# Narrow scores for the second half of the keys in a retention and MoE kernel, and the turns of two units moved

## The chip, the cores and the metric

The kernel runs on one core of a Trainium2 chip. The core has five engines with a queue each: TensorE (PE, matmuls, whose weight loads are listed apart as PEld), VectorE (DVE), ScalarE (ACT), GpSimd (POOL) and SyncE (SP, which here only issues DMAs). DMA transfers are carried out by 16 DMA engines, whichever queue issued them. The metric is the device time of one execution in microseconds (us), as the median of several; lower is better.

## The reference

The reference computes a retention layer and, on its result, a two-layer network with the ELU function between the layers.

```python
scores = scale * np.matmul(q, k.transpose(0, 1, 3, 2))       # q, k, v: 8 batches, 8 heads, 576 tokens, 64 wide
rel = pos[:, None] - pos[None, :]
Dmat = np.where(rel >= 0, gamma[:, None, None] ** rel[None, :, :], 0.0)
ret = np.matmul(scores * Dmat[None], v)                      # each query sees only keys at or before it
...
h = x @ w_in                                                 # x: ret as 4608 tokens x 512; w_in 512 x 2048
g = np.where(h > 0.0, h, np.exp(np.minimum(h, 0.0)) - 1.0)
out = g @ w_out                                              # w_out 2048 x 512
```

What matters for the change is the mask: a key that lies after a query contributes nothing to it.

## The kernel before

**Units.** The 4608 tokens are cut into 36 units of 128 tokens. Nine units cover two batches, so that the unit with `u % 9 == 4` holds the last 64 tokens of one batch and the first 64 of the next. The decay factors are split in two, one multiplied onto v (`scale_v`, on GpSimd, line 183) and one multiplied onto the result (`put_x`, on VectorE, line 316). What is left of the decay matrix inside a unit is a triangle of ones, and what earlier units contribute goes through a running state of 64 x 64 per head.

**Steps of a unit.** `load_v` and `load_qk` fetch the inputs. `turn(u)` transposes queries and keys so that the head width lies on the partitions. For units below `PE_TURNED` (8 of them) it does so with eight TensorE transposes into the buffer of the pool `ps_s`, from which VectorE copies one half (line 205) and ScalarE the other (line 206); for later units it is one DMA transpose on the SP queue (line 208). `scores(u)` (line 220) multiplies keys with queries, 16 matmuls in four groups, one for each pair of heads `hp`. The four matmuls of a group belong to the two heads `i` (rows 0 to 63 or 64 to 127 of the array) and the two halves `j` of the keys (columns 0 to 63 or 64 to 127). `masks(u)` (line 232) multiplies the scores with the triangle on VectorE. `inter(u)` (line 254) adds what the state contributes, `intra(u)` (line 303) what the unit's own keys contribute, `state(u)` (line 270) forms the unit's own addition to the state, and `state_out` (lines 285 to 295) adds it to the running sum on VectorE and casts it on ScalarE. These products share one buffer `o` of the pool `ps_o`, which there is once; the scores of a unit share the one buffer of `ps_s` with the transposes. `put_x` writes the unit's input of the network.

**The network.** Units are put together to groups: [0, 1, 2], [3], [4], [5], [6, 7], [8, 9], [10, 11, 12], [13, 14, 15] and fours after that. `ffn1` (called `f1`) computes one or more tiles of the first layer (line 382) into one of three buffers of `ps_h`. ELU is made by three engines in turn: the exponential e on ScalarE (line 387), m on GpSimd (line 389), and g on VectorE (line 347), which also frees the `ps_h` buffer. `ffn2` computes a quarter of an output tile (line 407).

**Order.** The order on each engine is that of the program text (`manual_schedule`), and only data and buffers make an engine wait. Up to unit 5 the order is written out by hand. After that a list of slots (tiles of `f1` and quarters of `ffn2`) is walked, and events are put between them by due times: `stretch(u)` (scores of the next unit, then `inter`, `intra`, `state` of the next unit, `put_x`), the turn of unit u + 3, and the loads of unit u + 5. A slot counter goes on with each slot (`tick`); things in `todo` are run when the counter has reached their number, and the g operations are run up to three slots late (`finish`). `dummy(n)` is n matmuls of 512 columns on a constant tile whose result is not used.

Of the kernel before, what the change touches and what calls it, by code (L numbers as in the profile page):

```python
# [9 lines left out]
FP32 = mybir.dt.float32  # L10
# [7 lines left out]
def kernel(  # L18
# [9 lines left out]
    nc = tc.nc  # L28
# [4 lines left out]
    P = 128  # L33
    HP = H // 2
# [8 lines left out]
    GROUPS += [list(range(u, u + 4)) for u in range(16, NU, 4)]  # L43
    NG = len(GROUPS)
    group_of = {u: (g, i) for g, us in enumerate(GROUPS) for i, u in enumerate(us)}
    PE_TURNED = 8

    def place(u):

# [22 lines left out]
    ps_s = ctx.enter_context(tc.tile_pool(name="ps_s", bufs=1, space=PSUM))  # L72
# [53 lines left out]
    for h in range(H):  # L126
        b, j = divmod(h, KJ)
# [40 lines left out]
    def dummy(n):  # L168

        if n:  # L170
            dum = ps_m.tile([P, 512], FP32, name="dum", tag="pm")
        for _ in range(n):
            nc.tensor.matmul(dum, warm[:, :P], warm, start=True, stop=True)  # L173


    qkTs, vns, scs, pts, os_, sbs, sts, sums = {}, {}, {}, {}, {}, {}, {}, {}

    def scale_v(u, half=None):

        if u not in vns:  # L180
            vns[u] = nat.tile([P, H, D], BF16, name="vn", tag="vn")
        h0, h1 = (0, H) if half is None else (half * HP, half * HP + HP)
        nc.gpsimd.tensor_tensor(  # L183
            vns[u][:, h0:h1], raws[u][:, h0:h1],
            gk[:, u % R, h0:h1].unsqueeze(2).to_broadcast([P, h1 - h0, D]), ALU.mult,
        )

    def turn(u, bank=None, keys_on_v=False, between=0):

        t = tpool.tile([P, 2, HP, P], BF16, name="qkT", tag="qkT")  # L190
        n = kns[u]
        c_v = 1 if keys_on_v else 0
        if u < PE_TURNED:
            if bank:
                pool, tag = bank
                ps = [pool.tile([P, HP, P], BF16, name="tr", tag=tag) for c in range(2)]
            else:
                both = ps_s.tile([P, 2, 2, HP, P], BF16, name="tr", tag="sc")
                ps = [both[:, c, 0] for c in range(2)]
            for c in range(2):  # L200
                if c:
                    dummy(between)
                for hp in range(HP):
                    nc.tensor.transpose(ps[c][:, hp], n[:, c, 2 * hp : 2 * hp + 2].rearrange("p h d -> p (h d)"), ident)  # L204
            nc.vector.tensor_copy(t[:, c_v], ps[c_v])
            nc.scalar.copy(t[:, 1 - c_v], ps[1 - c_v])  # L206
        else:
            nc.sync.dma_start_transpose(
                t.rearrange("p c h t -> p (c h) t"), n.rearrange("p c h d -> p (c h d)")
            )  # L210
        qkTs[u] = t

    def scores(u):
        t = qkTs[u]
        sc = ps_s.tile([P, 2, HP, P], FP32, name="sc", tag="sc")
        for hp in range(HP):
            for j in range(2):
                for i in range(2):
                    r = slice(i * D, (i + 1) * D)
                    nc.tensor.matmul(  # L220
                        sc[j * 64 : (j + 1) * 64, i, hp], t[r, 1, hp, j * 64 : (j + 1) * 64], t[r, 0, hp],
                        start=(hp == 0), stop=(hp == HP - 1), skip_group_check=True,
                    )
        scs[u] = sc

    def masks(u, i=None):

        if u not in pts:
            pts[u] = ppool.tile([P, 2, HP, P], BF16, name="pt", tag="pt")
        m = mask[:, 1 if u % R == 4 else 0]  # L230
        s = slice(0, 2) if i is None else slice(i, i + 1)
        nc.vector.tensor_tensor(  # L232
            pts[u][:, s].rearrange("p i h t -> p (i h) t"), scs[u][:, s].rearrange("p i h t -> p (i h) t"),
            m.unsqueeze(1).to_broadcast([P, (s.stop - s.start) * HP, P]), ALU.mult,
        )
# [5 lines left out]
    def inter(u):  # L241

        if u not in os_:
            os_[u] = ps_o.tile([P, 2, 512], FP32, name="o", tag="o")
        o = os_[u]
        r = u % R
        if r == 0:
            return
        n = 64 if r == 4 else P
        for a in range(2):  # L250
            for b in range(2):
                for i in range(2):
                    rows = slice(i * D, (i + 1) * D)
                    nc.tensor.matmul(  # L254
                        o[b * D : (b + 1) * D, i, a * P : a * P + n], sbs[u][rows, 2 * b + a],
                        qkTs[u][rows, 0, 2 * b + a, :n],
                        start=(a == 0), stop=False, skip_group_check=True,
                    )

    def state(u, beside):  # L260

        r = u % R
        if r == 8:
            return
        sts[u] = os_[beside][:, 1 if r == 4 else 0, 256:512].rearrange("p (c d) -> p c d", c=HP)
        rows = slice(64, P) if r == 4 else slice(0, P)
        for hp in range(HP):
            for i in range(2):
                h = 2 * hp + i
                nc.tensor.matmul(  # L270
                    sts[u][i * D : (i + 1) * D, hp], kns[u][rows, 1, h], vns[u][rows, h],
                    start=(hp == 0), stop=(hp == HP - 1), skip_group_check=True,
                )

    slot = [0]
    todo = []

    def state_out(u, cast_later=False):
        r = u % R
        if r == 8:  # L280
            return
        s = ppool.tile([P, HP, D], BF16, name="sb", tag="sb")
        sbs[u + 1] = s
        if r in (3, 7):
            nc.vector.tensor_tensor(s, sts[u], sums[u - 1], ALU.add)
            return
        sums[u] = ppool.tile([P, HP, D], FP32, name="sum", tag="sum")
        if r in (0, 4):
            nc.vector.tensor_copy(sums[u], sts[u])
        else:  # L290
            nc.vector.tensor_tensor(sums[u], sts[u], sums[u - 1], ALU.add)
        if cast_later:
            todo.append((slot[0] + 1, lambda: nc.scalar.copy(s, sums[u])))
        else:
            nc.scalar.copy(s, sums[u])

    def intra(u):
        o = os_[u]
        for a in range(2):
            for i in range(2):  # L300
                for b in range(2):
                    h = 4 * b + 2 * a + i
                    nc.tensor.matmul(  # L303
                        o[b * D : (b + 1) * D, i, a * P : (a + 1) * P], vns[u][:, h], pts[u][:, i, 2 * b + a],
                        start=(u % R == 0 and a == 0), stop=(a == 1), skip_group_check=True,
                    )
# [3 lines left out]
    def put_x(u):  # L310
        g, i = group_of[u]
        if i == 0:
            xts[g] = xpool.tile([P, KJ, 512], BF16, name="xt", tag="xt")
        r = u % R
        s0 = P * r if r < 5 else 64 + P * (r - 5)
        nc.vector.tensor_tensor(  # L316
            xts[g][:, :, i * P : (i + 1) * P].rearrange("p (a i) t -> p a i t", a=2), outputs(os_[u]),
            gx[:, :, s0 : s0 + P].rearrange("p (a i) t -> p a i t", a=2), ALU.mult,
        )

    def stretch(u, ahead=True):

        ahead = ahead and u + 1 < NU
        if ahead:
            scores(u + 1)
        inter(u)
        intra(u)
        if ahead:
            state(u + 1, u)
        put_x(u)  # L330
        if u + 2 < PE_TURNED:
            masks(u + 1)
        elif ahead:
            todo.append((slot[0] + 1, lambda: masks(u + 1)))
        if ahead:
            todo.append((slot[0] + 3, lambda: state_out(u + 1, True)))

# [5 lines left out]
    def finish(n=0):  # L343

        while late and late[0][0] <= slot[0] - n:
            _, gt_, ph, m, _ = late.pop(0)
            nc.vector.scalar_tensor_tensor(gt_, ph, 0.0, m, ALU.max, ALU.min)  # L347
# [129 lines left out]
    for u in range(2):  # L477
# [7 lines left out]
        state_out(u)  # L485
        dummy(2)
    scores(2)
    masks(2)
    dummy(4)


    def f1(g, n, bank=None):
        k = 512 // (P * len(GROUPS[g]))
        ffn1(g, k * n, bank)
# [61 lines left out]
    scores(5)  # L556
    state(5, 4)
    masks(5)
    f1(2, 0)
    f1(2, 1)  # L560
    finish(1)
    turn(6)
    scale_v(7)
    f1(2, 2)
    state_out(5)
# [32 lines left out]
    for u in range(5, NU):  # L598
        def at(share):
            return due[u] + share * (due[u + 1] - due[u])  # L600
        events.append((due[u], 0, u))
        if u + 2 < PE_TURNED:
            events.append((at(0.5), 1, u + 2))
# [7 lines left out]
    for f, g, s, d in slots:  # L611
        while events and events[0][0] <= now + d / 2:
            _, kind, u = events.pop(0)
# [13 lines left out]
    u = NU - 1  # L627
# [31 lines left out]
```

## Time and profile before

| | |
|---|---|
| time, median of 6 runs | 311.94 us (311.4 to 312.97) |
| the profiled execution | 312.79 us, of which the span of the profile is 311.0 us |
| busy in the span | PE 302.3, POOL 202.2, DVE 179.7, ACT 124.6, PEld 164.9 us |
| scores, L220 PE | 576 matmuls of 64 x 128, 15.0 us busy |
| transposes, L204 PE | 64 matmuls, 5.2 us busy |
| dummies, L173 PE | 34 matmuls, 11.0 us busy |
| DMA transposes, L208 SP | 28, median 4.7 us from issue to landing |

In the profile L220 is line 220 of the kernel. "pt<-sc,mask" reads: the operation writes `pt` and reads `sc` and `mask`. A timeline row has its start, the time that the row takes, the engine, the line, the operation, and in brackets how long the engine was idle before and what ended the idle time. A row of waits has the total, the number of times and the longest. A row of windows has the stretch, its length, the busy time and number of instructions of each engine named, the granted clock of TensorE as a share, the DMA busy time in the stretch and the rate in GB/s. Busy times of single matmuls overlap, since matmuls are pipelined.

### The profile page before, as it was taken

The numbers are of one execution on the slowest core, as the hardware profiler recorded it, in microseconds if no ns is written. First come the engines' busy times: TensorE is split into PE (matmuls) and PEld (weight loads), VectorE is DVE, ScalarE is ACT, GpSimd is POOL, SyncE is SP. The second block draws the span as 40 slices with busy tenths as digits, with TensorE's granted clock in tenths as the row PEclk, the third lists the DMA queues.
The fourth block names the chain that finished last, engine by engine and source line by source line (L and its number), as shares of the span: only waits on it lengthen the run. The fifth ranks groups of instructions, "written<-read, shape, count | busy, mean of one in ns | idle before, by whom it ended". The sixth has DMA issues, their size and how long they took to land.

```text
span 311.0 us, 7378 instructions
## 1 busy us (share of the span) xinstructions
PE 302.3 (97%) x2938; PEld 164.9 (53%) x2938; DVE 179.7 (58%) x305; ACT 124.6 (40%) x229; POOL 202.2 (65%) x292
## 2 busy tenths in 40 slices
PE   8897999899999999999999999999999999999995
PEld 3474746677666555555454444444444444444444
DVE  4657615776776666666666565666666665434300
ACT  5344413434434452344444433444334433444311
POOL 8886794899977778787777666766664433333300
PEclk9999999999999999999999999999999999999999
DMA  9999999799999999999999999999995200001111
GB/s 157 190 203 205 153 168 233 99 168 179 205 173 190 134 119 169 155 146 138 142 169 116 135 134 134 138 130 136 135 137 84 70 36 35 34 36 40 63 70 67
DMA packets 150882, 40.59 MB, mean 131 GB/s; under 512 B 141824, under 2 KB 146304, under 8 KB 150848
## 3 DMA queue, kind: packets, MB, share of 16 engines
q0 software_dynamic: 77264, 13.64, 56.0%
q1 hardware_dynamic: 72144, 24.19, 42.0%
q10 hardware_dynamic: 1440, 2.29, 2.2%
q8 instruction: 23, 0.38, 0.5%
q14 instruction: 11, 0.09, 0.1%
HBM read 36.70 MB, written 9.44 MB: 148 GB/s over the span
## 4 chain that ended last, share of the span: by engine, by line
PE 87%; DMA 6%; POOL 3%; DVE 1%; issue 1%; ACT 1%; POOLq 0%; DVEq 0%; ACTq 0%
PE ph L382 37%; PE pm L407 34%; PE pm L438 4%; PE o L303 4%; PE sc L220 4%; DMA w_in_sb<-in_moe_w_in_dram 4%; DMA qkn<-in_k_dram 3%; PE o L270 1%; POOL qkn L93 1%; PE pmh L423 1%; PE o L254 1%; PE tr L204 1%; POOL m L389 0%; DVE g L347 0%; DVE pt L232 0%
## 5 line engine op out<-in xcount | busy, mean ns | idle before, releaser
L389 POOL TENSOR_SCALAR m<-e 128x512 bf16<-128x512 f32 (+1 forms) x156 | 91.1, 586 | 89.2 <-ACT e L387 81.9
L382 PE MATMUL ph<-xt,w_in_sb 128*128 128x512 bf16 (+3 forms) x808 | 141.5, 313 | 2.2 <-DMA w_in_sb<-in_moe_w_in_dram 1.8
L387 ACT ACTIVATE e<-ph 128x512 f32<-128x512 f32 (+1 forms) x156 | 87.5, 564 | 137.6 <-PE ph L382 132.3
L347 DVE SCALAR_TENSOR_TENSOR g<-ph,m 128x512 bf16<-128x512 f32 (+1 forms) x156 | 99.7, 647 | 62.1 <-POOL m L389 61.8
L407 PE MATMUL pm<-w_out_sb,g 128*128 128x512 bf16 x496 | 125.5, 379 | 0.2 <-ACT ot L414 0.2
L382 PEld LDWEIGHTS <-w_in_sb 128*128 128x128 bf16 x808 | 69.2, 98 | 54.2 <-issue 3.0
L407 PEld LDWEIGHTS <-g 128*128 128x128 bf16 x496 | 48.0, 98 | 53.1 <-issue 0.4
L316 DVE TENSOR_TENSOR xt<-o,gx 128x512 bf16<-128x512 f32 x36 | 24.9, 691 | 39.6 <-PE o L270 30.6
L232 DVE TENSOR_TENSOR pt<-sc,mask 128x1024 bf16<-128x1024 f32 (+1 forms) x37 | 43.9, 1187 | 3.9 <-PE sc L220 3.9
L183 POOL TENSOR_TENSOR vn<-rv,gk 128x512 bf16<-128x512 f32 (+1 forms) x37 | 37.8, 1021 | 0.0
L93 POOL DMA_DIRECT2D qkn<-in_q_dram x39 | 35.1, 901 | 0.7 <-DVE pt L232 0.4
L93 POOL DMA_DIRECT2D qkn<-in_k_dram x39 | 33.3, 855 | 1.2 <-DMA qkn<-in_k_dram 1.2
L414 ACT COPY ot<-pm 128x512 f32<-128x512 f32 x31 | 18.1, 585 | 14.1 <-PE pm L407 14.1
L220 PEld LDWEIGHTS <-qkT 64*64 64x64 bf16 x576 | 9.2, 106 | 14.1 <-issue 10.8
L220 PE MATMUL sc<-qkT 64*64 64x128 bf16 x576 | 15.0, 222 | 0.9 <-ACT qkT L206 0.8
L303 PE MATMUL o<-pt,vn 128*64 128x128 bf16 x288 | 14.9, 225 | 0.0
L438 PE MATMUL pm<-w_out_sb,g 128*128 128x512 bf16 x64 | 14.5, 379 | 0.0
L173 PE MATMUL dum<-warm 128*128 128x512 bf16 x34 | 11.0, 457 | 1.2 <-DVE warm L119 1.2
L206 ACT COPY qkT<-tr 128x512 bf16<-128x512 bf16 x8 | 4.7, 583 | 15.5 <-DVE rv L82 10.7
L303 PEld LDWEIGHTS <-vn 128*64 128x64 bf16 x288 | 9.1, 109 | 3.0
L438 PEld LDWEIGHTS <-g 128*128 128x128 bf16 x64 | 6.1, 98 | 6.6
L270 PE MATMUL o<-vn,qkn 128*64 128x64 bf16 (+1 forms) x256 | 9.5, 196 | 0.0
(49 smaller groups left out, 98.1 us busy)
## 6 DMA issues: line engine op xcount, KB each, us to landing
rv<-in_v_dram SPq DMA_DIRECT2D x31, 256.0 KB, 4.9
out_dram<-ot SPq DMA_DIRECT2D x27, 256.0 KB, 2.4
qkn<-in_q_dram POOLq DMA_DIRECT2D x31, 128.0 KB, 5.0
qkn<-in_k_dram POOLq DMA_DIRECT2D x31, 128.0 KB, 5.4
w_in_sb<-in_moe_w_in_dram POOLq DMA_DIRECT2D x8, 256.0 KB, 9.3
w_out_sb<-in_moe_w_out_dram POOLq DMA_DIRECT2D x2, 1024.0 KB, 16.8
out_dram<-ot ACTq DMA_DIRECT2D x8, 256.0 KB, 3.9
rv<-in_v_dram SPq DMA_DIRECT2D x8, 128.0 KB, 5.4
```

What stands on the lines that cost most here:

```text
L93: nc.gpsimd.dma_start(kns[u][p0 : p0 + n, c], (q, k)[c][b, :, s0 : s0 + n, :].rearrange("h p d -> p h d"))
L183: nc.gpsimd.tensor_tensor(vns[u][:, h0:h1], raws[u][:, h0:h1], gk[:, u % R, h0:h1].unsqueeze(2).to_broadcast([P, h1 - h0, D]), ALU.mult,)
L220: nc.tensor.matmul(sc[j * 64 : (j + 1) * 64, i, hp], t[r, 1, hp, j * 64 : (j + 1) * 64], t[r, 0, hp], start=(hp == 0), stop=(hp == HP - 1) ...
L232: nc.vector.tensor_tensor(pts[u][:, s].rearrange("p i h t -> p (i h) t"), scs[u][:, s].rearrange("p i h t -> p (i h) t"), m.unsqueeze(1).t ...
L303: nc.tensor.matmul(o[b * D : (b + 1) * D, i, a * P : (a + 1) * P], vns[u][:, h], pts[u][:, i, 2 * b + a], start=(u % R == 0 and a == 0), s ...
L316: nc.vector.tensor_tensor(xts[g][:, :, i * P : (i + 1) * P].rearrange("p (a i) t -> p a i t", a=2), outputs(os_[u]), gx[:, :, s0 : s0 + P] ...
L347: nc.vector.scalar_tensor_tensor(gt_, ph, 0.0, m, ALU.max, ALU.min)
L382: nc.tensor.matmul(ph[:, i * n : (i + 1) * n], w_in_sb[:, j, f : f + P], xts[g][:, j, :n], start=(j == 0), stop=(j == KJ - 1), skip_group_ ...
L387: nc.scalar.activation(e[:, w], ph[:, w], AF.Exp)
L389: nc.gpsimd.tensor_scalar(m[:, w], e[:, w], -1.0, 1.0, ALU.add, ALU.mult)
L407: nc.tensor.matmul(pm, gts[g, ft][:, it * P : (it + 1) * P], w_out_sb[:, ft], start=(ft == 0), stop=(ft == NFT - 1))
L438: nc.tensor.matmul(acc[u], gts[g, ft][:, it * P : (it + 1) * P], w_out_sb[:, ft], start=(ft == 0), stop=(ft == NFT - 1))
```

## The change

`PE_TURNED` goes from 8 to 7. From unit 7 on, the scores of all units use one buffer of `ps_s` that is kept; its corner for the second 64 keys and the first 64 queries is zeroed once by VectorE (`keep_scores`, two slots after the stretch of unit 5). The matmuls of the second 64 keys are given the last 64 queries alone, so that eight of the 16 matmuls of a unit have 64 columns instead of 128. The mask of unit 6 is put one slot later. In the part written by hand, the turn of unit 6 is placed one slot sooner, between the two first tiles of group 2, and the turn of unit 7, which was an event after the stretch of unit 5 with TensorE transposes, becomes a DMA transpose ahead of the first of these tiles. Of four dummies after the mask of unit 2, one stays.

```diff
-    PE_TURNED = 8
+    PE_TURNED = 7
...
     def scores(u):
         t = qkTs[u]
-        sc = ps_s.tile([P, 2, HP, P], FP32, name="sc", tag="sc")
+        narrow = u >= PE_TURNED
+        if narrow:
+            sc = scs[PE_TURNED]
+        else:
+            sc = ps_s.tile([P, 2, HP, P], FP32, name="sc", tag="sc")
         for hp in range(HP):
             for j in range(2):
                 for i in range(2):
                     r = slice(i * D, (i + 1) * D)
+                    c = slice(j * 64 if narrow else 0, P)
                     nc.tensor.matmul(
-                        sc[j * 64 : (j + 1) * 64, i, hp], t[r, 1, hp, j * 64 : (j + 1) * 64], t[r, 0, hp],
+                        sc[j * 64 : (j + 1) * 64, i, hp, c], t[r, 1, hp, j * 64 : (j + 1) * 64], t[r, 0, hp, c],
                         start=(hp == 0), stop=(hp == HP - 1), skip_group_check=True,
                     )
         scs[u] = sc
+
+    def keep_scores():
+
+        scs[PE_TURNED] = ps_s.tile([P, 2, HP, P], FP32, name="sc", tag="sc")
+        nc.vector.memset(scs[PE_TURNED][64:P, :, :, 0:64], 0.0)
...
         elif ahead:
             todo.append((slot[0] + 1, lambda: masks(u + 1)))
+        if u + 2 == PE_TURNED:
+            todo.append((slot[0] + 2, keep_scores))
         if ahead:
             todo.append((slot[0] + 3, lambda: state_out(u + 1, True)))
...
     scores(2)
     masks(2)
-    dummy(4)
+    dummy(1)
...
     masks(5)
+    turn(7)
     f1(2, 0)
+    turn(6)
     f1(2, 1)
     finish(1)
-    turn(6)
     scale_v(7)
```

## The prediction

> **What bounds the kernel now.** I read the chain that ended last first, then TensorE's waits.
>
> ```profile
> PE 87%; DMA 6%; POOL 3%; DVE 1%; issue 1%; ACT 1%; POOLq 0%; DVEq 0%; ACTq 0%
> ```
>
> ```profile
> PE ph L382 <- DMA w_in_sb<-in_moe_w_in_dram: 1.8, 1, 1.8
> ...
> PE sc L220 <- ACT qkT L206: 0.8, 1, 0.8
> PE tr L204 <- DMA qkn<-in_k_dram: 0.7, 1, 0.7
> PE ph L382 <- DVE g L347: 0.4, 1, 0.4
> ```
>
> After about 30 us the end is set by TensorE (PE) working without pause; its named waits come to some 5 us, most of them early. So an edit counts if it shortens TensorE's own sequence after 30 us or removes a wait there. Hence three places: the scores of each unit, the dummies near 16 us, the turns of units 6 and 7 near 55 us.
>
> The scores of unit 24, in stretches of 56 ns, line 220 alone (microseconds, TensorE's busy time and matmuls touched, then weight loads):
>
> ```profile
> 169.62:169.70 0.08, 0.07 (x4) 0.07 (x8) 1.00 0.00 0
> 169.70:169.76 0.06, 0.06 (x8) 0.06 (x12) 1.00 0.00 0
> 169.76:169.81 0.06, 0.06 (x12) 0.06 (x12) 1.00 0.00 0
> 169.81:169.87 0.06, 0.06 (x16) 0.06 (x8) 1.00 0.00 0
> ```
>
> Four more of the 16 matmuls are touched in each stretch: the quads (two row halves i by two column halves j) run side by side, one quad per 56 ns.
>
> TensorE by hand-off around the two turns, then the timeline of the helpers there:
>
> ```profile
> 54.27:56.33 2.06, 2.06 (x35) 1.00 0.28 98
> 56.33:57.11 0.78, 0.00 (x0) 1.00 0.00 0
> 57.11:58.04 0.93, 0.93 (x40) 1.00 0.06 15
> ...
> 59.81:60.11 0.30, 0.16 (x3) 1.00 0.15 25
> 60.11:60.56 0.45, 0.44 (x8) 1.00 0.66 22
> ```
>
> ```profile
> 54.76 0.62 POOL L389 TENSOR_SCALAR m<-e 128x512 bf16<-128x512 f32 x1 [0.27 <-ACT e L387]
> ...
> 55.42 0.69 DVE L347 SCALAR_TENSOR_TENSOR g<-ph,m 128x512 bf16<-128x512 f32 x1 [0.20 <-POOL m L389]
> 56.02 0.41 DVE L205 COPY qkT<-tr 128x512 bf16<-128x512 bf16 x1
> 56.36 0.41 DVE L291 TENSOR_TENSOR sum<-o,sum 128x256 f32<-128x256 f32 x1
> ...
> 56.47 0.58 ACT L206 COPY qkT<-tr 128x512 bf16<-128x512 bf16 x1 [1.79 <-DVE qkT L205]
> ```
>
> Unit 6's transposes are done by 54.4, but VectorE (DVE) copies them only at 56.02, behind two g operations; ScalarE (ACT) copies the other half after that, and the scores of unit 6 start at 57.11 after 0.78 us of idle. The next row to note is the sum at 56.36: it reads the state out of the product buffer `o`, of which there is one, so `inter(5)` may not write `o` before it.
>
> **What the Trainium skill says.** "TensorE: Matmul & The Clock Gate", section Back-to-back issue gap, gives columns/2.4 + 2.5 ns between warm matmuls: 56 ns for 128 columns, 29 for 64. The trace agrees: 56 per quad above, and 32 for pairs of the 64-column state products. "TensorEngine Tiling (Array Packing)", Key Properties: tiles work independently, and a change of tiling mode drains the engine; here a quad starts within 10 ns, and the first scores matmul follows the last 512-column one by 308 ns instead of 216. "PSUM — Partial Sum Buffer", The four PSUM rules: VectorE writes leave the accumulation bits alone, and a matmul sets bits only on the columns it addresses; so a corner zeroed once stays zero, without cost for later units. No run here shows that yet. "VectorE: DVE Perf Modes", Zero memsets, has a memset at one cycle per element; the memset of `warm` (256 elements) took 0.272 us, so 512 are 0.54 us by the trace.
>
> **Part 1: narrow scores, units 7 to 35.** 29 units, each with 8 of 16 matmuls cut from 128 to 64 columns. If columns added up, that were 29 x 8 x 27 ns = 6.2 us. But each quad holds two j=0 matmuls that still stream 128 columns, and the next quad begins on those same tiles. The period stays 56 ns; the short half only ends sooner beside the long one. After the fourth quad comes the first of `inter` on a j=0 tile, or a mode change that waits for the later of both. I take 0. Bounds: nothing lost (no instruction is added), gained at most 4 quads x 27 ns x 29 = 3.1 us if the pace were that of the short ones. Also 26 of TensorE's waits on its own older work go; the gap of 308 ns is the mode change (product to first layer shows the same 92 ns extra), so 0 too.
>
> **Part 2: dummies 4 to 1.** Three 512-column matmuls at 216 ns: 0.65 us of TensorE at 15.4 to 16.3. They are in front of two gates that don't move:
>
> ```profile
> 18.36 0.91 POOL L108 DMA_DIRECT2D w_out_sb<-in_moe_w_out_dram  x1 [0.60 <-DMA w_in_sb<-in_moe_w_in_dram]
> 19.63 0.88 POOL L108 DMA_DIRECT2D w_out_sb<-in_moe_w_out_dram  x1 [0.35 <-DMA w_in_sb<-in_moe_w_in_dram]
> 20.53 1.94 POOL L389 TENSOR_SCALAR m<-e 128x384 bf16<-128x384 f32 x4
> ```
>
> GpSimd (POOL) issues the output weights until 20.51 and only then takes m, whose g frees TensorE's buffers at 21.70 (0.37 us of wait, about 1.0 after the change). Behind that TensorE waits 1.75 us for the last input weights, whose transfer was issued at 17.14 and landed at 28.18. Worth 0. Without this cover it would be 0.65 gained. The other end is a loss through the clock: the wait before 21.70 grows to 1 us while 1.75 us at 28 leaves the granted clock at 1.0, so I put that at nothing.
>
> **Part 3: unit 6's turn one slot sooner, unit 7 by DMA.** Removed from TensorE: unit 7's transposes, 59.81 to 60.56, with their wait for the mask of unit 6, 0.75 us; one DVE copy (0.41) and one ACT copy (0.58) go too. Step by step from 52 us, with latencies of this trace:
> - `f1(2,0)` ends its 16 matmuls at 52.93. Unit 6's transposes need the buffer that the mask of unit 5 reads until 53.13, so they start at 53.18: a new wait of 0.25. They take 0.44; `f1(2,1)` runs from 53.62 (before: 52.93).
> - DVE copies at 53.85 (0.28 after the last transpose), ACT from 54.30 (0.45 after DVE's start) to 54.88. This stands in front of the exponential of `f1(2,1)`, which moves from 54.09 to about 54.80.
> - Hence m at 55.48 (+0.68), g at 56.13 (+0.65), the sum at 56.74 (+0.61), done at 57.15. The old gate was the ACT copy; the new one is this sum, queued behind the late g.
> - TensorE reaches the scores of unit 6 at 56.40 instead of 57.11, but `inter(5)` waits for the sum and starts at 57.21; before, at 57.36. Of 0.71 gained, 0.15 is left.
> - Then the removed 0.75: the scores of unit 7 would come 0.9 sooner, at 61.53. DVE now has put_x(5) at 58.00, g at 58.61, the late mask of unit 6 at 59.21 (1.13), g at 60.35, the memset at 60.95 (0.52 to the next), sum at 61.47, done 61.88. `inter(6)` waits for that sum: 61.94 against 62.67, so 0.73 is left. With a memset as slow as g (0.61 to the next) it is 0.64.
> - POOL does m, then v of unit 7 (1.04), then m of `f1(2,2)`: 57.04 against 57.64. It is then busy 8.27 of the 8.5 us from 57.5 to 66, so the m, g and put_x(7) after it come 0.60 sooner and no more. Before, `f1(4,0)` followed put_x(7) at once, at 68.68; now at 68.08.
>
> From there all is as before, 0.60 us sooner; TensorE has no long wait until the end. Unit 7's DMA transpose can go out on the SP queue at 51.3, when its keys have landed (51.24), before the v load of unit 9 (56.87). It takes 1.3 us of the queue and, by the median of the 28 others, 4.7 to landing; the scores need it at 61.5. Its traffic falls in a hole: the DMA share is 0.28 of 2.06 us from 54.27 on and zero from 56.33 to 57.11. The loads of unit 9 go out 0.6 sooner with m.
>
> Sum: 0 + 0 - 0.60. The profiled execution had a span of 311.0 us within 312.79; that becomes 310.4 within 312.2. Its time is 0.85 over the median of the six, 311.94; from the median I get 311.3.
>
> **Rivals.**
> 1. *The chain behind unit 6's ACT copy is not late* (the exponential slips in first, or the g and sum find other slack). Then TensorE keeps 0.71 + 0.75 = 1.46: 310.5. For it: only 0.1 to 0.2 us decide at several of these steps. Against it: ACT takes work in order, and the copy stands first. Chance 0.18.
> 2. *Narrow scores do pay*, the short half setting part of the pace: up to 3.1 on top, about 309 with half of it. Against it is the count of four per 56 ns. Chance 0.12.
> 3. *All is absorbed*, POOL and DVE being the gate: TensorE's 0.60 goes at a later wait such as the masks near 118 us, and 311.9 stays. Chance 0.13.
> 4. *Slower, by DMA.* The key load of unit 9 landed at 65.46, its transpose at 71.15 and its scores started at 72.26: a slack of 1.11, all other units having 3.8 or more. If the added transpose pushes these loads, TensorE waits. With 0.60 gained first it costs from a delay of 0.5 on, and the kernel is slower than before from 1.1 on; a delay of 2.2 (one more transpose ahead of both the load and the turn) gives 313.0. Against it is the hole. Chance 0.07.
>
> **How the numbers follow.** The forecast has 0.50. A measurement of this kernel tells about 0.3% (0.94 us) from no change. Faster by that are rivals 1 and 2 and some 0.04 of the forecast: 0.34. Slower is rival 4: 0.07. Within: 0.59. The range takes in rivals 1 and 3 with the spread of the measured times, 310.3 to 312.2, and leaves out most of 2 and 4. The forecast's own range is 310.9 to 311.7.
>
> **What would show it.** In the changed kernel: scores quads still 56 ns apart; a longer wait for g near 21.7; no idle ahead of unit 6's scores, but one of 0.6 us behind them, ended by a DVE sum; m of `f1(2,2)` near 57.0; `f1(4,0)` near 68.1. Wrong would be quads closer than 56 ns, the weights landing at another time than 28.2, or unit 9's scores waiting for DMA.

## The result and the profile after

The changed kernel takes 311.53 us in the median of 35 runs (310.05 to 314.94), against 311.81 us in the median of 72 runs of the kernel before (310.88 to 314.61). The ratio is 0.9987, with an interval of 0.9975 to 0.9999: some 0.4 us less, within the 0.3% that the prediction called no change. The profiled execution of the changed kernel took 311.53 us, with a span of 309.7 us.

First the chain that ended last, of the kernel after:

```profile
PE 86%; DMA 5%; POOL 4%; DVE 2%; issue 1%; ACT 1%; POOLq 0%; DVEq 0%; ACTq 0%
```

It is still TensorE that carries the end. Its own waits have changed. From the list of waits of the kernel after (total, times, longest, in us):

```profile
PE sc L227 <- DMA qkT<-qkn: 1.0, 1, 1.0
...
PE ph L396 <- DVE g L361: 0.7, 1, 0.7
...
PE o L266 <- DVE rv L82: 0.4, 1, 0.4
...
PE sc L227 <- DVE sc L236: 0.2, 1, 0.2
```

The 0.8 us for ScalarE's copy ahead of unit 6's scores, and 1.8 us for the last input weights, are no longer among them. Four others stand there: scores that wait for a DMA transpose (1.0), a longer wait for g (0.7 instead of 0.4), a wait of `inter` for DVE (0.4; the operation named, on line 82, is a marker of 0.06 us right behind the sum, which is what was waited for), and one for the zeroing (0.2).

The span is 1.3 us shorter than before, but it must not be read as what the change gave. The timeline of TensorE after, just ahead of the point from which it runs without a pause:

```profile
26.55 1.46 PE L396 MATMUL ph<-xt,w_in_sb 128*128 128x384 bf16 x8
27.94 0.32 PE L282 MATMUL o<-vn,qkn 128*64 128x64 bf16 x8
```

The tile at 26.55 is the one for which the kernel before waited until 28.31, because the last input weights landed at 28.18. Here they landed at 26.42. I therefore count from now on from the **gate**: the first product of unit 3, at 27.94 us here and at 29.70 us in the profile before. Everything behind it is a fixed sequence, and the same step comes at the same time behind the gate, within 0.01 us, in profiles of the same kernel, up to the first place where something is late. The gate itself stands 1.52 to 1.53 us behind the landing of the last input weights in all 13 profiles of this document. So one profile tells steps of 0.1 us apart, where the times of whole runs lie up to 4.9 us apart.

Counted so, the two turns stand as follows in the timeline after, from 50 us:

```profile
52.52 0.58 ACT L206 COPY qkT<-tr 128x512 bf16<-128x512 bf16 x1 [0.49 <-DVE qkT L205]
...
54.64 0.42 PE L227 MATMUL sc<-qkT 64*64 64x128 bf16 x16
...
54.96 0.41 DVE L303 TENSOR_TENSOR sum<-o,sum 128x256 f32<-128x256 f32 x1
...
55.42 0.31 PE L266 MATMUL o<-qkT,sb 64*64 64x128 bf16 x8 [0.37 <-DVE rv L82]
...
59.37 0.48 DVE L236 MEMSET sc<- 64x512 f32 x1
...
60.00 0.41 PE L227 MATMUL sc<-qkT 64*64 64x128 bf16 x16 [0.18 <-DVE sc L236]
```

Unit 6's scores (54.64) have no idle ahead of them, and 0.37 us behind them, ended by the sum. Idle time is counted from the modelled end of the matmul before; by the starts, `inter` comes 0.78 us behind the scores instead of 0.25 (57.11 to 57.36) in the kernel before, so the delay is 0.53 us. And there is a wait of 0.18 us for the zeroing ahead of unit 7's.

### The profile page after: what moved, and what is told of

It reads as the page before. It is cut to its first block, busy times and chain, and to the rows that moved or that the text cites. A ratio compares the mean times of both kernels' runs of the same rounds, so it can differ in the third digit from the quotient of the medians.

```text
span 309.7 us, 7359 instructions
## 1 busy us (share of the span) xinstructions
PE 300.9 (97%) x2927; PEld 163.8 (53%) x2927; DVE 179.6 (58%) x305; ACT 124.2 (40%) x228; POOL 202.4 (65%) x292
## 4 chain that ended last, share of the span: by engine, by line
PE 86%; DMA 5%; POOL 4%; DVE 2%; issue 1%; ACT 1%; POOLq 0%; DVEq 0%; ACTq 0%
PE ph L396 37%; PE pm L421 33%; PE pm L452 4%; PE o L315 4%; PE sc L227 3%; DMA w_in_sb<-in_moe_w_in_dram 3%; DMA qkT<-qkn 2%; PE o L266 1%; PE o L282 1%; POOL qkn L93 1%; PE pmh L437 1%; DVE g L361 1%; POOL w_in_sb L105 1%; DVE pt L244 1%; POOL vn L183 1%
## 5 line engine op out<-in xcount | busy, mean ns | idle before, releaser
L227 PE MATMUL sc<-qkT 64*64 64x128 bf16 (+1 forms) x576 | 14.8, 212 | 1.3 <-DMA qkT<-qkn 1.0
L266 PE MATMUL o<-qkT,sb 64*64 64x128 bf16 (+1 forms) x256 | 11.1, 216 | 0.4 <-DVE rv L82 0.4
L173 PE MATMUL dum<-warm 128*128 128x512 bf16 x31 | 9.9, 447 | 1.2 <-DVE warm L119 1.2
```

Of the source, the lines that this page charges most:

```text
L227: nc.tensor.matmul(sc[j * 64 : (j + 1) * 64, i, hp, c], t[r, 1, hp, j * 64 : (j + 1) * 64], t[r, 0, hp, c], start=(hp == 0), stop=(hp == H ...
```

## The experiments

All of them are read by the time from the gate to five places: scores of unit 6, of unit 8 and of unit 9, the start of the last matmul, and the end of the span. The last column is the delay of unit 9's scores by their DMA transpose: how much later they start than 0.20 us behind the matmul before them, which is the step where nothing is late (the profile's rows of waits count from modelled ends and show 0.1 us less). In us:

| kernel | gate at | unit 6 | unit 8 | unit 9 | last matmul | end of span | delay of unit 9 |
|---|---|---|---|---|---|---|---|
| before, first profile | 29.70 | 27.41 | 37.27 | 42.55 | 277.83 | 281.32 | 0 |
| before, second | 29.30 | 27.41 | 37.26 | 42.65 | 277.94 | 281.42 | 0.12 |
| narrow scores alone | 28.50 | 27.41 | 37.31 | 42.75 | 277.86 | 281.54 | 0.09 |
| turns alone | 29.27 | 26.69 | 36.35 | 43.11 | 278.40 | 281.87 | 1.16 |
| after, first profile | 27.94 | 26.69 | 36.69 | 43.03 | 278.13 | 281.80 | 1.06 |
| after, second | 28.97 | 26.69 | 36.69 | 42.55 | 277.66 | 281.32 | 0.61 |
| after, third | 28.06 | 26.69 | 36.69 | 41.94 | 277.04 | 280.71 | 0 |
| after with four dummies | 28.73 | 26.70 | 36.69 | 41.94 | 277.05 | 280.72 | 0 |
| after, loads of unit 9 early | 28.70 | 26.70 | 36.69 | 41.94 | 277.05 | 280.71 | 0 |
| after, state's sum early | 29.76 | 26.70 | 36.51 | 41.94 | 277.05 | 280.72 | 0 |
| first further version | 28.55 | 26.69 | 36.15 | 41.41 | 276.61 | 280.27 | 0 |
| second further version | 29.04 | 26.69 | 36.16 | 41.41 | 276.61 | 280.28 | 0 |
| after, all scores short | 28.62 | 26.69 | 37.22 | 42.38 | 275.05 | 278.71 | 0 |

From the start of the last matmul to the end of the span it takes 3.47 to 3.49 us in the three profiles without narrow scores and zeroing (the two before and the turns alone) and 3.66 to 3.68 us in the ten with them. By the records of the trace it is VectorE's last closing step that comes later there, with 3.4 to 3.5 us behind the last matmul instead of 3.0; why is not known. These 0.19 us belong to the time of a run, so a gain read at the last matmul is that much too large for every kernel with the zeroing.

### Narrow scores alone

```diff
-    PE_TURNED = 7
+    PE_TURNED = 8
...
-    dummy(1)
+    dummy(4)
...
-    turn(7)
     f1(2, 0)
-    turn(6)
     f1(2, 1)
     finish(1)
+    turn(6)
```

(against the changed kernel; the scores are narrow from unit 8 on)

> The narrow scores alone (from unit 8, four dummies, turns of units 6 and 7 as before). Theory A (the two halves run side by side, and the long half sets 56 ns per quad): the quads stay 56 ns apart, time within 0.3 us of the kernel before. Rival (columns add up, or the short half sets part of the pace): quads at 42 ns or less, 1.5 to 3 us faster.

Measured: 311.9 us in 14 runs against 312.16, ratio 0.9993 (0.9978 to 1.0009). The run is too coarse for it, but the trace isn't. From the scores of unit 11 to those of unit 35 the kernel before takes 173.02 us, this one 172.87, and the changed kernel with all its parts 172.87 too: 0.15 us over 24 units, 6.5 ns for each. The prediction had 0. Nothing of it reaches the last matmul in this kernel (277.86 against 277.83): by the products behind unit 8's scores 0.12 us are lost, most likely to the zeroing, which here ends on VectorE 0.15 us ahead of these scores as it does ahead of unit 7's in the kernel after, and 0.09 at unit 9's transpose. How this comes about is seen in the changed kernel at unit 24, first in stretches of some 56 ns (TensorE's busy time and matmuls touched, then weight loads; the last three numbers of such a row are the granted clock, the busy share of the DMA engines, which is not a time, and GB/s):

```profile
168.24:168.30 0.06, 0.05 (x4) 0.06 (x8) 1.00 0.00 0
168.30:168.35 0.05, 0.05 (x10) 0.05 (x14) 1.00 0.00 0
168.35:168.41 0.06, 0.06 (x14) 0.06 (x15) 1.00 0.00 0
168.41:168.46 0.05, 0.05 (x16) 0.05 (x8) 1.00 0.00 0
```

and then TensorE's timeline of the same place:

```profile
168.25 0.35 PE L227 MATMUL sc<-qkT 64*64 64x128 bf16 x14
...
168.40 0.22 PE L266 MATMUL o<-qkT,sb 64*64 64x128 bf16 x2
...
168.44 0.22 PE L227 MATMUL sc<-qkT 64*64 64x128 bf16 x2
```

The counts are no longer 4, 8, 12, 16 but 4, 10, 14, 16. The single records of the trace, which these rows merge, show why: from the second quad on the short matmuls of the half j=1 start 32 ns apart (168.305, 168.337, 168.369), the long ones of j=0 still 56 ns apart (168.326, 168.382, 168.438). The short half runs ahead, and the first products of `inter` (168.40) even start before the last long scores (168.44). But the long half sets the end, and almost all of what the short half gains is waited for.

### All scores short

```diff
-                    c = slice(j * 64 if narrow else 0, P)
+                    c = slice(j * 64, (j + 1) * 64) if narrow else slice(0, P)
...
-        nc.vector.memset(scs[PE_TURNED][64:P, :, :, 0:64], 0.0)
+        nc.vector.memset(scs[PE_TURNED], 0.0)
```

(against the changed kernel) This leaves out, from unit 7 on, the scores of the last 64 queries with the first 64 keys, which the result needs.

> Scores of the first 64 keys cut to the first 64 queries too, which leaves out a quarter of the scores that are needed; all 16 matmuls have 64 columns. Theory A (the pace of a quad is set by its 128-column half): quads 28 to 32 ns apart instead of 56, each unit about 0.1 us shorter between scores, 2 to 3 us over units 7 to 35. Rival (the pace is issue or weight loads): no more than the 6.5 ns per unit of the narrow scores.

Measured: one run of 309.19 us, against 312.14 before. From unit 11 to unit 35 it takes 170.71 us, 90 ns less for each unit than the changed kernel. TensorE's timeline at unit 24 of this kernel:

```profile
166.92 0.32 PE L227 MATMUL sc<-qkT 64*64 64x64 bf16 x16
167.07 0.28 PE L266 MATMUL o<-qkT,sb 64*64 64x128 bf16 x8
```

`inter` begins 0.15 us behind the first scores, instead of 0.25 in the kernel before (169.63 to 169.88). So 64 columns less are worth 24 ns for each quad (90 and 6.5 ns over four quads), close to the 27 of the prediction's bound, but only when both halves lose them.

### The turns alone

```diff
-    PE_TURNED = 8
+    PE_TURNED = 7
...
     masks(5)
+    turn(7)
     f1(2, 0)
+    turn(6)
     f1(2, 1)
     finish(1)
-    turn(6)
```

(against the kernel before)

> The moved turns alone (unit 6 one slot sooner, unit 7 by DMA, mask of unit 6 one slot later; full scores, four dummies, no zeroing). Theory A (the turns are all of the change; the chain of exponential, m, g and sum leaves 0.6 us, and unit 9's DMA transpose then lands too late and takes some of it back): 0 to 0.6 us faster, with a wait of TensorE for a DMA transpose at unit 9's scores of 0.5 to 1.2 us. Rival (the wait for unit 9 in the changed kernel's profile was one execution's accident): no such wait, 0.6 us faster.

Measured: 312.63 us in 14 runs against 312.16, ratio 1.0004 (0.9982 to 1.0027). Without the zeroing the gain at unit 8 is 0.92 us (37.27 to 36.35), and then it is lost twice. From the waits of this kernel:

```profile
PE sc L220 <- DMA qkT<-qkn: 1.1, 1, 1.1
...
PE ph L382 <- DVE xt L316: 0.2, 1, 0.2
```

The first-layer tile behind `put_x(7)` waits 0.2 us for it, and the scores of unit 9 wait 1.1 us for their transpose. Without that they would stand at 41.94, as in the third profile after. The last matmul comes 0.57 us later than in the first profile before.

### Four dummies again

```diff
-    dummy(1)
+    dummy(4)
```

(against the changed kernel)

> The changed kernel with four dummies again. Theory A (the last input weights' landing gates TensorE near 26 to 28 us whatever the dummies are, and the 1.76 us between the two profiles is scatter of that landing): same time as the changed kernel, within 0.3 us; the landing is at 26 to 28 us. Rival (fewer dummies let the weights land sooner): landing again near 28.2, and 0.5 to 1.7 us slower than the changed kernel.

Measured: 311.74 us in 22 runs against 312.16, ratio 0.9993 (0.9977 to 1.0009). Behind the gate it agrees to 0.01 us with the third profile of the changed kernel. Its wait for g near 21.7 is 0.4 us; over the profiles at hand that wait is 0.28 to 0.81 with four dummies (five profiles, mean 0.47) and 0.7 to 1.7 with one (eight, mean 1.07): TensorE comes earlier and waits longer for the same g. The last input weights land at 28.18, 27.78, 26.98, 27.75 and 27.20 with four dummies, and between 26.42 and 28.23 with one. The gate is at 29.10 in the mean of the five and at 28.71 in the mean of the eight. With a scatter of half a microsecond in either group that difference isn't settled; no run shows that the dummies move it.

### The loads of unit 9 early

```diff
+    load_qk(9)
     turn(7)
     f1(2, 0)
...
     state_out(5)
-    load_qk(9)
```

(against the changed kernel)

> The changed kernel with the q and k loads of unit 9 issued ahead of the turn of unit 7 instead of after the state of unit 5. Theory A (unit 9's transpose lands late because these loads wait on GpSimd behind m of f1(2,2), and DMA is full): TensorE's wait at unit 9's scores (1.0 us) is gone, and the kernel is 0.6 to 1.2 us faster than the changed kernel. Rival (the added DMA transpose itself makes everything late): the wait stays or moves to unit 8 or 10, no gain.

Measured: 311.51 us in 14 runs against 312.16, ratio 0.999 (0.9965 to 1.0015). Unit 9's transpose is there 2.8 us before it is needed, and the last matmul comes at 277.05, 1.08 sooner than in the first profile after. This shows that the whole of that profile's loss behind unit 8 is the late transpose of unit 9. In whole runs the expected 0.6 to 1.2 us against the changed kernel do not appear (311.51 against 311.53 and, in another comparison, 312.01). Such medians are too coarse for it, and the wait to be removed differs between executions of the changed kernel, as the next section shows.

### The same two kernels again

> The changed kernel once more, unaltered, for a second profile and beside the version with the early sum. Theory A (its own gain is steady, and what varies is the wait for unit 9's transpose and the landing of the last input weights): from the first product of unit 3 to the scores of unit 8 again 36.69 us; the scores of unit 9 between 41.94 (no wait) and 43.1. Rival (the gain itself is scatter): the stretch to unit 8 differs by over 0.1 us.

> The kernel before once more, unaltered, for a second profile. Theory A: from the first product of unit 3 to the last matmul 277.8 us again, the landing of the last input weights anywhere from 26.4 to 28.2, and unit 9's transpose close to its scores (within 1.2 us). Rival (the late landing at 28.2 belongs to the kernel before): 28.2 again.

> The changed kernel once more, for a third profile. Theory A: unit 8's scores 36.69 us after the first product of unit 3 again, unit 9's between 41.94 and 43.1 depending on when its transpose lands.

Measured: the changed kernel 312.01 us in 22 runs against 312.14, ratio 0.9999 (0.9981 to 1.0017), and one run of 310.54 in a later comparison with 312.24; the kernel before one run of 312.53. Up to unit 8 the three profiles after agree to 0.01 us. At unit 9 they part: a wait of 1.1, 0.6 and none. The two profiles before part there too, a little: none and 0.10. The instructions that touch `qkT` on the SP queue from 56 to 71 us, before and then after, end in this row (minimum, median and maximum of three transposes, from issue to landing):

```profile
DMA to landing us min/median/max: 5.0/5.5/6.3
```

```profile
DMA to landing us min/median/max: 6.4/6.9/7.6
```

Unit 9's own transpose took 5.5 and 6.3 us in the two profiles before and 6.4 with the narrow scores alone. With the turns moved it took 7.6, 7.0 and 6.1 in the three profiles after, 5.7 with four dummies and 7.5 with the turns alone. It is sent out 0.3 to 1.1 us sooner behind the gate (35.2 to 35.6 against 35.9 to 36.3), while the scores need it 0.61 sooner. So the slack is no larger than the scatter in either kernel, and the duration of one transfer decides. The second and third profile after come from two different chips, so how much of that scatter lies between chips and how much between executions on one chip is not separated. For unit 8's transpose, just before, the difference is steady: 5.0, 5.4 and 5.3 us in the three profiles with the turns as before, 6.3 to 6.8 in the eight with the turns moved (the two further versions left out), and it lands 1.4 to 2.3 us ahead of its scores instead of 4.1 to 4.5. So the moved turns do lengthen that transfer, by 1.3 us in the mean; unit 8 had the slack for it.

### The state's sum early

```diff
     f1(2, 0)
     turn(6)
+    state_out(5, True)
     f1(2, 1)
...
     f1(2, 2)
-    state_out(5)
```

(against the changed kernel: the sum that `inter(5)` waits for is put right behind unit 6's copies)

> The changed kernel with the sum of unit 5's state moved right behind unit 6's copies, and nothing else. Theory A (that sum, late behind g, holds unit 5's products): the 0.57 us of idle behind unit 6's scores is gone and unit 7's scores come 0.3 to 0.57 us sooner than 32.05 us after the first product of unit 3; GpSimd's order then still holds put_x of unit 7, so unit 9's scores come no sooner than 41.8 us, or later where its transpose is late. Rival (something else holds unit 5's products): unit 7's scores at 32.05 again.

Measured: one run of 312.25 us. The idle behind unit 6's scores is gone, but unit 7's scores come only 0.18 us sooner, not 0.3 to 0.57 as expected, and unit 9's not at all. Its timeline says what came in its place:

```profile
60.99 0.48 DVE L236 MEMSET sc<- 64x512 f32 x1
...
61.62 0.41 PE L227 MATMUL sc<-qkT 64*64 64x128 bf16 x16 [0.55 <-DVE sc L236]
```

TensorE could go on 0.56 us earlier, but the zeroing, which is placed by the slots and stands behind a g, starts only 0.20 us sooner (31.23 behind the gate instead of 31.43) and holds it for 0.37 us more. After that the first-layer tile that needs `put_x(7)` comes at 38.37 behind the gate, as in the third profile after, so the 0.18 is lost there. Removing one link of this chain lets the next one bind.

### Two further versions

The first takes up three things: the loads of unit 9 early, the state's sum early, and narrow scores (and so the zeroing) from unit 14 on only.

```diff
+    NARROW = 14
...
-        narrow = u >= PE_TURNED
+        narrow = u >= NARROW
...
+    load_qk(9)
     turn(7)
     f1(2, 0)
     turn(6)
+    state_out(5, True)
     f1(2, 1)
...
-    state_out(5)
-    load_qk(9)
```

(against the changed kernel; `keep_scores` moves with `NARROW`)

> The changed kernel with three edits: the sum of unit 5's state right behind unit 6's copies on VectorE instead of behind two g; the loads of unit 9 ahead of unit 7's turn; narrow scores and their zeroing only from unit 14. Theory A (unit 5's products wait for that sum, the zeroing stands in front of unit 6's sum, and unit 9's loads are late): counted from the first product of unit 3 to the last matmul the kernel before has 277.83 us; 277.83 - 0.71 - 0.75 - 22 x 0.0065 = 276.2, 0.85 less than the best profile of the changed kernel's parts so far (277.05), and the idle behind unit 6's scores is gone. Rival (GpSimd's order of m and v holds the pace anyway): 276.9 to 277.1, the idle appears in front of a first-layer tile.

Measured: 311.56 us in 22 runs against 312.14, ratio 0.9981 (0.996 to 1.0002); last matmul 276.61, where 276.2 was expected. With two loads ahead of it, unit 7's transpose took 8.7 us from issue to landing, and its scores waited 0.3 us. So the second version puts the loads between the tiles:

```diff
-    load_qk(9)
     turn(7)
     f1(2, 0)
+    load_qk(9, 0)
     turn(6)
     state_out(5, True)
     f1(2, 1)
+    load_qk(9, 1)
```

> As the version with the early sum, but the two loads of unit 9 go out between and behind the first two m of group 2 instead of ahead of unit 7's turn, where they made that turn's transpose take 8.7 us. Theory A (with early loads and early sum only the order on the DMA engines is left): unit 7's scores no longer wait for DMA (0.3 us in that version), and from the first product of unit 3 to the last matmul 276.2 to 276.4 us instead of 276.61. Rival (the DMA engines are full whatever the order): a wait of as much at unit 7, 8 or 9.

Measured: 310.94 us in 22 runs against 312.24, ratio 0.9967 (0.9948 to 0.9985): by the ratio 1.03 us faster than the kernel before (0.47 to 1.62). The wait of unit 7's scores is gone, but the last matmul is at 276.61 once more, not at 276.2 to 276.4. From the timeline of this version:

```profile
60.31 0.41 DVE L306 TENSOR_TENSOR sum<-o,sum 128x256 f32<-128x256 f32 x1
...
60.87 0.31 PE L269 MATMUL o<-qkT,sb 64*64 64x128 bf16 x8 [0.17 <-DVE sum L306]
```

What unit 7 gained is now waited for behind its scores, for the sum of unit 6. At the last matmul that is 1.28 us less than the mean of the two profiles before, and at the end of the span 1.09 (281.37 to 280.28), which the measured 1.03 fits.

## Why the prediction was right, and where it wasn't

**The sum, 311.3 us.** Measured 311.53, and by the ratio about 0.41 us gained (0.03 to 0.78) where 0.60 was forecast. The later comparison of the same two kernels, at a ratio of 0.9999, has 0.03 us gained (from 0.59 gained to 0.53 lost), so the gain is known no better than as a few tenths. The size is right within its own range of 310.9 to 311.7, and it is made up of a gain that was predicted, of a loss that stood only in rival 4, and of two terms that nearly cancel: the narrow scores and the longer close. That they add up to a number so near is in part luck. Two of the prediction's three signs of being wrong appeared, the last weights landing at another time than 28.2 and unit 9's scores waiting for DMA, and the third in half: the short matmuls are 32 ns apart, the long ones still 56.

**Part 1, narrow scores, taken as 0.** The long half does keep 56 ns, as argued. But the step "the next quad begins on those same tiles" took the pair of halves to go on together. They don't: each half keeps its own pace, and the short one reaches `inter` earlier. Measured 6.5 ns for each unit, 0.19 us for 29 units, well below the bound of 3.1. Nor was "nothing lost (no instruction is added)" right: the zeroing, which the prediction counted only in part 3, is added, it holds TensorE once, and the close of the span is 0.19 us longer in all ten profiles that have the zeroing and the narrow scores. To the end of the span the narrow scores so come to about 0, but not for the reason given. Rival 2 (half of that bound) is ruled out by it, and the run with both halves short shows what it would have needed.

**Part 2, dummies, taken as 0.** The wait for g grew by about as much as the dummies shrank (0.65 us): from 0.37 to 0.71 in the two first profiles, and by 0.60 in the means over all. The gate is the landing of the last input weights, as predicted. "Two gates that don't move" was wrong for the second one in a way that the first profile couldn't show: that landing moves, by 1.2 us among the five profiles with four dummies and by 1.8 among the eight with one.

**Part 3, the turns, -0.60.** The prediction's own times less the gate of the profile before (29.70), and the first profile after less its gate (27.94), in us:

| step | before | predicted | measured |
|---|---|---|---|
| ACT copy for unit 6 | 26.77 | 24.60 | 24.58 |
| g of `f1(2,1)` | 25.72 | 26.43 | 26.41 |
| sum of the state | 26.66 | 27.04 | 27.02 |
| scores of unit 6 | 27.41 | 26.70 | 26.69 |
| `inter(5)` | 27.66 | 27.51 | 27.48 |
| m of `f1(2,2)` | 27.94 | 27.34 | 27.36 |
| zeroing | | 31.25 | 31.43 |
| scores of unit 7 | 32.72 | 31.83 | 32.05 |
| `inter(6)` | 32.97 | 32.24 or 32.33 | 32.37 |
| `f1(4,0)` | 38.98 | 38.38 | 38.39 |

The chain behind ScalarE's copy, the exponential, m, g and the sum, came as written, so rival 1 is out. One step was off. The zeroing starts 0.79 us behind the g before it instead of the 0.60 taken, so 0.18 late, and it holds unit 7's scores; the prediction had let it hold only `inter(6)`. That costs 0.34 us at unit 8, which is 0.58 sooner in all three profiles and 0.92 with the turns alone, but nothing at unit 9: there the step on GpSimd's pace holds, with 0.61 us sooner wherever the transpose is in time, and the turns alone come to the same (43.11 less the delay of 1.16), after their wait for `put_x(7)`.

**Rival 4, the DMA, given 0.07.** The wait that it names is what happened, with a smaller price. The step that failed is "from there all is as before, 0.60 us sooner". It rested on unit 9's slack of 1.11 us, which was one landing in one execution; the second profile before has 0.04. And the hole in the DMA traffic from 54 to 57 us is no cover for a transfer that runs from 63 to 71. Measured: delays of 1.06, 0.61 and 0 in the three profiles after, and 0 with four dummies; 0.42 in the mean of these four, against 0.07 for the three profiles with the turns as before. (The variant with the early sum has 0 too, but there the transpose is sent out 34.3 us behind the gate, sooner than in the others.) With that, -0.61 for the turns, -0.18 for the narrow scores of the 27 units from 9 on, +0.19 for the longer close and +0.35 for the delays make -0.25, inside the interval, though a mean of four such delays is itself rough. Why a given transpose takes 5.7 us in one execution and 7.6 in another was not settled. No run adds unit 7's DMA transpose without moving unit 6's turn, so how much of the longer landing is its doing, as rival 4 had it, stays open.

**Rival 3, all absorbed.** Not so: in the third profile 0.79 us goes through to the last matmul (277.04 against 277.83), of which 0.18 are the narrow scores, and 0.61 to the end of the span (280.71 against 281.32). In the first profile it was absorbed and more, but by a DMA, not by the pace of GpSimd and VectorE.

## What to carry to other kernels

A slack read from one profile is one draw when its end is a transfer: take the landing times of all like transfers (here 4.6 to 7.6 us for the same transpose) and ask whether the gained time is still covered by the slow ones. When the head of a kernel ends in such a landing, compare profiles from a point behind it, not by their spans, and follow them to the end of the span: a stretch behind the last matmul that looks the same can differ. And where matmuls run side by side on halves of the array, shortening one half is worth almost nothing: look for the reduction that shortens both.

## What was not expected of the hardware

TensorE's two column halves keep separate pace in 64 x 64 tiles, and starts fall out of program order. The Trainium skill, "TensorE: Matmul & The Clock Gate", section The mechanism (packing small matmuls), has matmuls in program order in start and end. In the traces of the narrow scores a short matmul starts at 168.305 ahead of an earlier long one at 168.326, and a product of `inter` at 168.40 ahead of scores at 168.44. For starts the measurement decides; ends are modelled in the profile and say nothing here. "TensorEngine Tiling (Array Packing)", Key Properties, which has tiles work independently, is what the trace agrees with. The zeroing of 64 x 512 elements took 0.48 us, 0.94 ns for each element of a partition, where 0.54 us had been estimated.
